# Attention scores from split q and k, with the transposes two steps behind, in a fused attention and feed-forward kernel

## The chip, the cores and the metric

The kernel runs on one core of a Trainium2 chip. The metric is device time in microseconds (us) of one execution. Three runs of the kernel before gave a median of 1192.46 us, between 1191.99 and 1193.89.

## What is computed

Attention over 4 batches and 8 heads of 576 positions and 64 dimensions with a learned bias of the relative position, and then two feed-forward parts over its 2304 x 512 result. All inputs are float32.

```python
def attn(q, k, v, w1, b1, w2):                  # (4, 8, 576, 64)
    scores = q @ k.T / 8
    x = log1p(abs(i - j)) / log1p(max(i, 1))
    bias = relu(x * w1 + b1) @ w2               # one 576 x 576 plane a head
    attn = softmax(scores + bias)
    return attn @ v
def moe1(x, w_in, w_out):                       # 512 -> 2048 -> 512
    h = x @ w_in
    return (h * cos(h)) @ w_out
def moe2(x, w_gate, w_val, w_out, rms_g):       # 512 -> 1536 -> 512
    xn = x / sqrt(mean(x * x) + 1e-6) * rms_g
    g = xn @ w_gate
    return (g * sigmoid(g) * (xn @ w_val)) @ w_out
```

## The kernel before

The program has three stages in one instruction order, which is written out by hand: each engine executes its instructions in the order in which the code issues them, and waits for the tiles of the others.

**Bias stage** (to about 72 us). In 36 steps T, VectorE (and ScalarE for one of some four) makes the hidden features `ft` of 16 positions (`features`, L413), TensorE multiplies them with w2, and the planes go to DRAM. Steps 0, 1 and 2 of the first attention unit lie at T = 28, 31 and 35 (`STEP_AT`).

**Attention** (to about 332 us). A unit u is a pair of heads and a batch, 16 in all, with five steps p (`step`, L328). Steps 0 to 3 treat 128 queries of both heads, step 4 the last 64 queries of both. `qk` multiplies q and k in float32 into one PSUM tile `psS` a head; there are two such tiles (L212). In steps 0 to 3 the two heads sit on different halves of TensorE's rows, so their instructions run in pairs; a float32 instruction shows as two in the trace. `softmax` adds the bias and takes the row minimum on VectorE (L231, here called a reduction), which frees the tile, and ScalarE takes the exponential (L235). `tr(u, p - 1)` then transposes the exponentials of the step before: four blocks that ScalarE copies out, four that VectorE copies out (L248) and a last one (L251, copied at L252), in PSUM tiles `pt` of three buffers. `av` multiplies five chunks of v with the transposed exponentials, for a half of the queries at a time (half 0: 256, half 1: 320), into the single PSUM tile `o`. `recip` makes the reciprocals of the sums (L287, L288), and GpSimd spreads them over `rw` (L290). `norm` transposes them on TensorE into a PSUM tile of the same three buffers (L298), and ScalarE copies them to `rbc` (L300). `norm_out` multiplies `o` with them on VectorE (L313), which frees `o`, and splits the result: ScalarE rounds it to `xh` (L315), GpSimd subtracts to get the rest, `xl` (L316).

**Feed-forward parts.** All products are of three rounded ones (`mm3`): the high part with the high, the high with the low, the low with the high part. The work is cut into items n: 80 of the first part (16 blocks of 128 features by 5 blocks of tokens) and 60 of the second (12 by 5). Item n makes its features, and item n - 2 (`LAG`) multiplies its own with the output weights.

**Weights.** They come as float64 in 68 pieces. A piece passes `w_dma`, `w_abs` (ScalarE, L105), `w_conv` (VectorE, in two halves of two instructions each: L116 and L117, L120 and L121) and `w_split` (ScalarE rounds at L137, GpSimd subtracts at L138) into a slot of a ring. Conversions are placed in steps 0 and 3 of the units from 4 on, and behind the items. `w_tick` decides what may be issued after a step or an item, from what was already done one call earlier:

```python
128         j = i % (WA + WB)
...
153         i = wstate["abs"]
154         if i < wstate["dmad"] and i < wstate["splitd"] + NW32:
155             w_abs()
```

The ring has WA + WB = 10 slots (`wA`, `wB`), and NW32 = 6 converted pieces may lie ahead of the splitting. `ready` issues all that is missing just ahead of the products that need it.

In a step the order of issue is: `norm_out` of the unit before (p 1 and 3), `qk`, `norm` (p 2 and 4), `softmax`, `tr`, `av`, loads of k and q for the next unit (p 1), and the conversion half (p 0 and 3).

Of the kernel before, what the change touches and what calls it, by code (L numbers as in the profile page):

```python
# [23 lines left out]
SPAN = 2 * S - 4  # L24
BLKS = [(0, 512), (512, 512), (2048, 256), (1024, 512), (1536, 512)]
# [5 lines left out]
WA = 1  # L31
WB = 9
NRAW = 2
NW32 = 6
# [17 lines left out]
def attn_moe(tc, qd, kd, vd, smallp, lrow, ident_d, wf1, wf2, rmsg, out):  # L52
# [117 lines left out]
    def load_k(u):  # L170
        if u < 16:
            hp, b = divmod(u, 4)
            kt = prep.tile([128, 640], F32, tag="k", name="kt", bufs=2)
            nc.sync.dma_start(kt, kd[b, hp])
            kq[u] = [kt, None]

    def load_q(u):
        if u < 16:
            hp, b = divmod(u, 4)
            qt_ = prep.tile([128, 640], F32, tag="q", name="qt", bufs=2)  # L180
            nc.sync.dma_start(qt_, qd[b, hp])
            kq[u][1] = qt_
# [24 lines left out]
    def qk(u, p):  # L207
# [15 lines left out]
        return [ps]
# [14 lines left out]
    def tr(u, p):  # L238
        s_ = st[u]
        e = s_["e"].pop(p)  # L240
        if p < 4:
            eT, q0 = (s_["eT0"], 128 * p) if p < 2 else (s_["eT1"], 128 * (p - 2))
            for c, ev in ((0, nc.scalar.copy), (2, nc.vector.tensor_copy)):
                pt = psA.tile([128, 512], F32, tag="tr", name="pt", bufs=3)
                for i in range(4):
                    k0 = 128 * (c + i // 2) + (S + 64) * (i % 2)
                    nc.tensor.transpose(pt[:, 128 * i:128 * i + 128], e[:, k0:k0 + 128], ident)  # L247
                ev(eT[:, 2 * c:2 * c + 4, q0:q0 + 128], pt.rearrange("p (c q) -> p c q", c=4))  # L248

            pt = psA.tile([128, 512], F32, tag="tr", name="pt", bufs=3)  # L250
            nc.tensor.transpose(pt[:, 0:128], e[:, 512:640], ident)  # L251
            nc.vector.tensor_copy(eT[:, 8, q0:q0 + 128], pt[:, 0:128])  # L252
        else:
            eT = s_["eT1"]
            pt = psA.tile([128, 512], F32, tag="tr", name="pt", bufs=3)
            for c in range(4):
                nc.tensor.transpose(pt[:, 128 * c:128 * c + 128], e[:, 128 * c:128 * c + 128], ident)  # L257
            nc.scalar.copy(eT[:, 0:8, 256:320], pt.rearrange("p (c q) -> p c q", c=8))
            pt = psA.tile([128, 512], F32, tag="tr", name="pt", bufs=3)
            nc.tensor.transpose(pt[:, 0:128], e[:, 512:640], ident)  # L260
# [545 lines left out]
```

## Time and profile before

| | |
|---|---|
| median of 3 runs | 1192.46 us |
| the profiled execution | 1192.12 us, span 1190.3 us |
| TensorE (PE) busy | 1173.7 us, 99% |
| VectorE (DVE) busy | 825.6 us, 69% |
| ScalarE (ACT) busy | 542.1 us, 46% |
| GpSimd (POOL) busy | 351.6 us, 30% |
| granted TensorE clock | full in all 40 slices |
| chain that ended last | PE 85%, DVE 8%, ACT 3%, issue 2%, DMA 1% |

The span is the time in which the profile saw the engines; the 1.8 us between it and the execution's own time lie around it. Busy shares are means over the three stages. The chain follows each piece of work back to what released it; its shares say which engine's work the end hung on. In the rows further below, an entry in square brackets is idle time just ahead of the instruction, and the instruction that ended it.

### The profile page before, as it was taken

Reading aid. Unit: us, or ns where it says so; the run is one execution under the profiler, and the core shown is the slowest. Engines: PE = TensorE matmul, PEld = TensorE weight load, DVE = VectorE, ACT = ScalarE, POOL = GpSimd, SP = SyncE. Lnnn points to the kernel's source line nnn. Section 1 sums busy time; section 2 is a strip of 40 time slices with the busy share of each in tenths; the row PEclk is TensorE's granted clock in tenths of the full one; section 3 lists DMA queues with packets and bytes.
Section 4 is the critical chain, followed back from the end, with each engine's and each line's share of the span. In section 5 each row is a group of like instructions: output and inputs, shape, how many; then the busy total and the mean of one; then the engine's idle time right before and its main releaser. Section 6 shows DMA issues by size and latency. Waiting matters only on the chain.

```text
span 1190.3 us, 17685 instructions
## 1 busy us (share of the span) xinstructions
PE 1173.7 (99%) x6628; PEld 907.4 (76%) x6628; DVE 825.6 (69%) x1588; ACT 542.1 (46%) x1060; POOL 351.6 (30%) x373
## 2 busy tenths in 40 slices
PE   7999999999999999999999999999999999999998
PEld 3466666666678888888888887888888888888887
DVE  8966677777778789879879987885565355533232
ACT  7966667767654444445435546332222222222111
POOL 0011112222232244234234445663331232123111
PEclk9999999999999999999999999999999999999999
DMA  6833425362212011201201110111112011200012
GB/s 194 267 120 108 135 66 160 103 191 65 69 37 70 19 36 36 71 19 37 70 18 43 46 36 18 50 58 36 36 36 74 16 46 43 71 1 1 36 46 78
DMA packets 30852, 79.23 MB, mean 67 GB/s; under 512 B 3888, under 2 KB 4144, under 8 KB 30768
## 3 DMA queue, kind: packets, MB, share of 16 engines
q1 hardware_dynamic: 30480, 77.52, 20.8%
q8 instruction: 52, 0.85, 0.3%
q10 hardware_dynamic: 288, 0.59, 0.1%
q14 instruction: 32, 0.26, 0.1%
HBM read 62.76 MB, written 15.34 MB: 66 GB/s over the span
## 4 chain that ended last, share of the span: by engine, by line
PE 85%; DVE 8%; ACT 3%; issue 2%; DMA 1%; POOL 0%; SPq 0%; DVEq 0%; ACTq 0%; POOLq 0%
PE y L508 25%; PE h L508 13%; PE hg L508 12%; PE hv L508 12%; PE o L278 7%; PE psS L217 6%; PE pt L247 5%; PE psS L222 1%; DVE ft L413 1%; PE psb L443 1%; ACT G L449 1%; DVE yacc L611 1%; PE pt L257 1%; PE rp L298 1%; PE pt L251 1%
## 5 line engine op out<-in xcount | busy, mean ns | idle before, releaser
L508 PE MATMUL y<-g,wB 128*128 128x512 f32 (+1 forms) x960 | 213.4, 370 | 1.7 <-DVE yacc L611 1.2
L508 PEld LDWEIGHTS y<-g,wB 128*128 128x128 f32 x960 | 167.6, 188 | 34.4 <-DVE yacc L611 2.8
L558 POOL TENSOR_TENSOR g<-t,g 128x512 fp32r<-128x512 f32 (+1 forms) x80 | 98.1, 1227 | 236.8 <-ACT g L557 236.8
L575 POOL TENSOR_TENSOR g<-t,g 128x512 fp32r<-128x512 f32 (+1 forms) x60 | 74.1, 1235 | 292.3 <-ACT g L574 292.3
L231 DVE CUSTOM_DVE_ANT_0 e<-psS,bias 128x576 f32<-128x576 f32 x144 | 103.8, 753 | 63.6 <-PE psS L217 47.7
L508 PE MATMUL h<-xh,wB 128*128 128x512 f32 (+1 forms) x480 | 145.4, 369 | 0.0
L508 PE MATMUL y<-wB,g 128*128 128x512 f32 x594 | 143.5, 390 | 0.0
L235 ACT ACTIVATE e<-e,sm 128x576 f32<-128x576 f32 x144 | 110.6, 769 | 53.1 <-DVE sm L231 53.1
L508 PE MATMUL hv<-xh,wB 128*128 128x512 f32 (+1 forms) x440 | 133.7, 369 | 0.0
L508 PE MATMUL hg<-xh,wB 128*128 128x512 f32 (+1 forms) x440 | 133.2, 368 | 0.4 <-DVE t L570 0.4
L570 DVE TENSOR_TENSOR t<-t,hg 128x512 f32<-128x512 f32 (+1 forms) x60 | 38.0, 633 | 137.4 <-ACT t L569 137.4
L508 PEld LDWEIGHTS y<-wB,g 128*128 128x128 f32 x594 | 110.8, 188 | 22.5
L569 ACT ACTIVATE t<-hg 128x512 f32<-128x512 f32 (+1 forms) x60 | 33.3, 554 | 168.0 <-PE hg L508 161.8
L574 ACT CAST g<-t 128x512 fp32r<-128x512 f32 (+1 forms) x60 | 34.7, 578 | 164.5 <-DVE t L573 164.5
L508 PEld LDWEIGHTS h<-xh,wB 128*128 128x128 f32 x480 | 87.8, 188 | 16.0 <-issue 0.5
L552 ACT ACTIVATE r<-r 128x512 f32<-128x512 f32 (+1 forms) x80 | 47.2, 590 | 108.0 <-DVE r L549 107.7
L278 PE MATMUL o<-eT,v 128*64 128x256 f32 (+1 forms) x640 | 94.3, 416 | 0.0
L508 PEld LDWEIGHTS hg<-xh,wB 128*128 128x128 f32 x440 | 80.5, 188 | 15.0 <-DVE t L570 0.9
L138 POOL TENSOR_TENSOR wB<-w,wB 128x512 fp32r<-128x512 f32 x61 | 85.2, 1403 | 21.4 <-ACT wB L137 21.4
L508 PEld LDWEIGHTS hv<-xh,wB 128*128 128x128 f32 x440 | 80.6, 188 | 13.7
L557 ACT CAST g<-t 128x512 fp32r<-128x512 f32 (+1 forms) x80 | 46.2, 578 | 96.3 <-DVE t L556 87.9
L508 PE MATMUL h<-xl,wB 128*128 128x512 f32 (+1 forms) x240 | 88.4, 368 | 0.0
(116 smaller groups left out, 2130.8 us busy)
## 6 DMA issues: line engine op xcount, KB each, us to landing
raw<-in_wf_dram SPq DMA_DIRECT2D x68, 512.0 KB, 3.5
bdram<-G SPq DMA_DIRECT2D x36, 288.0 KB, 3.6
bias<-bdram SPq DMA_DIRECT2D x32, 288.0 KB, 3.3
kt<-in_kd_dram SPq DMA_DIRECT2D x16, 320.0 KB, 4.5
qt<-in_qd_dram SPq DMA_DIRECT2D x16, 320.0 KB, 5.1
v<-in_vd_dram SPq DMA_DIRECT2D x16, 320.0 KB, 3.9
out_dram<-yacc SPq DMA_DIRECT2D x16, 256.0 KB, 2.1
bias<-bdram SPq DMA_DIRECT2D x4, 144.0 KB, 3.3
```

What stands on the lines that cost most here:

```text
L138: eng.tensor_tensor(t[:, 1, :], r, t[:, 0, :].bitcast(F32), op=ALU.subtract)
L217: nc.tensor.matmul(pss[hh][:, x, 0:288], qt_[r, 128 * p:128 * p + 128], kt[r, k0:k0 + 288], start=True, stop=True, tile_position=(64 * hh, 0))
L231: nc.vector.tensor_tensor_reduce(out=e.rearrange("p (a b) -> p a b", a=2), in0=ps[:, :, 0:288], in1=bias_t[j].rearrange("p (a b) -> p a b" ...
L235: nc.scalar.activation(e, e, AF.Exp, bias=s_["m"][:, j:j + 1], scale=-1.0, accum_out=s_["sum"][:, j:j + 1])
L247: nc.tensor.transpose(pt[:, 128 * i:128 * i + 128], e[:, k0:k0 + 128], ident)
L278: nc.tensor.matmul(o[64 * hh:64 * hh + 64, 0:n], vt[:, c, 64 * hh:64 * hh + 64], eT[:, 2 * c + (hh if c < 4 else 0), :], start=(c == 0), s ...
L508: nc.tensor.matmul(ps, a, b_, start=(first and k == 0), stop=(last and k == tot - 1))
L552: nc.scalar.activation(r, r, AF.Abs)
L557: nc.scalar.copy(g[:, 0, :tn], t)
L558: nc.gpsimd.tensor_tensor(g[:, 1, :tn], t, g[:, 0, :tn].bitcast(F32), op=ALU.subtract)
L570: nc.vector.tensor_tensor(t, t, pg, op=ALU.mult)
L575: nc.gpsimd.tensor_tensor(g[:, 1, :tn], t, g[:, 0, :tn].bitcast(F32), op=ALU.subtract)
```

## The change

- *Scores.* GpSimd splits k and q of the next unit into a rounded and a rest part (`split`: a cast and a subtraction over 128 x 640 each), k in step 2, q in step 3. `qk` then sums three rounded products. Unit 0 keeps its float32 products, and unit 1 is loaded and split at T = 2 of the bias stage.
- *Transposes.* `tr` is two steps behind the scores and cut in two: its first four transposes and ScalarE's copy ahead of the softmax, the rest behind it.
- *Reciprocals.* They are transposed into the free columns of the tile of the last transpose (steps 2 and 4), and VectorE copies them out instead of ScalarE. `norm_out` moves to steps 2 and 4, and `xt` has one buffer instead of two.
- *Products with v.* They follow in steps 4 (chunks 0 and 1), 0 (2 and 3) and 1 (4) for half 0, and in 2 (0 to 2) and 3 (3 and 4) for half 1.
- *Loads.* k and q of the next unit are issued in step 0.
- *Weights.* The ring keeps ten slots, of which three (`wC`) exist only from item 2 on; until then seven pieces may be split. NW32 is 5.

```diff
+TERMS = ((0, 0), (0, 1), (1, 0))
...
-WB = 9
+WB = 6
+WC = 3
+RING = WA + WB + WC
-NW32 = 6
+NW32 = 5
...
-        j = i % (WA + WB)
+        j = i % (WA + WB + WC)
...
+        elif j >= WA + WB:
+            t = wstate["wc"].tile([128, 2, 512], F32R, tag="w", name="wC", bufs=WC)
...
+    def load(u):
+        for k, src in enumerate((kd, qd)):
+            if u == 0:
+                t = rawp.tile([128, 512, 2], I32, tag="raw", name="first", bufs=NRAW)
+                t = t.rearrange("p a b -> p (a b)")[:, 0:640].bitcast(F32)
+                kq[0] = kq.get(0, []) + [t]
+            else:
+                t = prep.tile([128, 640], F32, tag="raw", name="raw" + "kq"[k], bufs=2)
+            nc.sync.dma_start(t, src[u % 4, u // 4])
+            raw_kq[u, k] = t
+
+    def split(u, k):
+        raw = raw_kq.pop((u, k))
+        t = prep.tile([128, 2, 640], F32R, tag="kq"[k], name="kq"[k] + "t", bufs=2)
+        nc.gpsimd.tensor_copy(t[:, 0, :], raw)
+        nc.gpsimd.tensor_tensor(t[:, 1, :], raw, t[:, 0, :].bitcast(F32), op=ALU.subtract)
+        kq[u] = kq.get(u, []) + [t]
...
         kt, qt_ = kq[u]
-        if p < 4:
...
+        terms = TERMS
+        if u == 0:
+            terms, kt, qt_ = ((0, 0),), kt.unsqueeze(1), qt_.unsqueeze(1)
+        pss = [psB.tile([128, 2, 512], F32, tag="S", name="psS", bufs=2) for _ in range(2 if p < 4 else 1)]
+        for x in range(2):
+            for n, (a, b_) in enumerate(terms):
+                for hh, ps in enumerate(pss):
+                    r = slice(64 * hh, 64 * hh + 64) if p < 4 else slice(0, 128)
...
+                    nc.tensor.matmul(ps[:, x, 0:288], qt_[r, a, 128 * p:128 * p + 128], kt[r, b_, k0:k0 + 288],
+                                     start=(n == 0), stop=(n == len(terms) - 1), tile_position=(64 * hh, 0))
+        return pss
...
-    def tr(u, p):
+    def tr(u, p, first, spread=None):
         s_ = st[u]
-        e = s_["e"].pop(p)
+        if first and p in (0, 2):
...
+        pt = psA.tile([128, 512], F32, tag="tr", name="pt", bufs=3)
+        if first:
+            for i in range(4):
+                k0 = 128 * (i // 2) + (S + 64) * (i % 2) if p < 4 else 128 * i
+                nc.tensor.transpose(pt[:, 128 * i:128 * i + 128], e[:, k0:k0 + 128], ident)
+            nc.scalar.copy(eT[:, 0:512 // n, q0:q0 + n], pt.rearrange("p (c q) -> p c q", q=n))
+            return
...
+            for i in range(4):
+                k0 = 128 * (2 + i // 2) + (S + 64) * (i % 2)
+                nc.tensor.transpose(pt[:, 128 * i:128 * i + 128], e[:, k0:k0 + 128], ident)
+            nc.vector.tensor_copy(eT[:, 4:8, q0:q0 + n], pt.rearrange("p (c q) -> p c q", q=n))
+        nc.tensor.transpose(pt[:, 0:128], e[:, 512:640], ident)
+        if spread is not None:
+            norm(*spread, pt[:, 128:384])
...
-    def norm(u, half):
+    def norm(u, half, rp):
         s_ = st[u]
-        rp = psA.tile([128, 512], F32, tag="tr", name="rp", bufs=3)
...
-        nc.scalar.copy(rbc[:, 0:256], rp[:, 0:256])
+        nc.vector.tensor_copy(rbc[:, 0:256], rp)
         s_["rbc", half] = rbc
...
-        xt = ap.tile([128, 320], F32, tag="xt", name="xt", bufs=2)
+        xt = ap.tile([128, 320], F32, tag="xt", name="xt", bufs=1)
...
-        if u > 0 and p in (1, 3):
-            norm_out(u - 1, p // 2)
+        if u > 0 and p in (2, 4):
+            norm_out(u - 1, p // 4)
-        if p == 2 and u > 0:
-            norm(u - 1, 1)
+        if p == 3 and u > 0:
             norm_tail(u - 1)
-        if p == 4:
-            norm(u, 0)
+        back = (u, p - 2) if p > 1 else (u - 1, p + 3)
+        if back[0] >= 0:
+            tr(*back, True)
...
-        if p > 0:
-            tr(u, p - 1)
+        if back[0] >= 0:
+            tr(*back, False, (u, 0) if p == 4 else (u - 1, 1) if p == 2 and u > 0 else None)
+        if p == 2:
+            recip(u, 0)
+        if p == 0 and u > 0:
+            recip(u - 1, 1)
+        if p == 4:
+            av(u, 0, [0, 1])
         elif u > 0:
-            tr(u - 1, 4)
-            av(u - 1, 0, [3, 4])
-        if p == 1 and u > 0:
-            av(u - 1, 1, [0, 1, 2])
-        if p == 2:
-        if p == 4:
-            av(u, 0, [2])
-        if p == 3:
-            av(u, 0, [0, 1])
+            av(u - 1, p // 2, ([2, 3], [4], [0, 1, 2], [3, 4])[p])
+        if p in (2, 3) and 0 < u < 15:
+            split(u + 1, p - 2)
+        if p == 0 and 0 < u < 15:
+            load(u + 1)
...
-        if T == 20:
-            load_k(1)
-        if T == 22:
-            load_q(1)
+        if T == 2:
+            load(1)
+            split(1, 0)
+            split(1, 1)
...
-        w_tick(lambda i: i < WA + WB or lastuse[pieces[i - WA - WB]] <= n - SPL,
+        w_tick(lambda i: i < WA + WB or n > 1 and (i < RING or lastuse[pieces[i - RING]] <= n - SPL),
                nsplit=2 if n < 6 or m == 2 else 1)
...
-    tr(15, 4)
+    tr(15, 3, True)
+    tr(15, 3, False)
     recip(15, 1)
-    av(15, 0, [3, 4])
+    av(15, 0, [2, 3, 4])
+    tr(15, 4, True)
+    tr(15, 4, False, (15, 1))
...
+    wstate["wc"], st_wc = pool("wc")
```

How this stands on TensorE, from step 4 of a unit through steps 0 and 1 of the next to the scores of step 2 (`psS` scores, `pt` transposes, `rp` reciprocals, `o` products with v). Before:

```order
L298 MATMUL rp<-ident,rw 128x128 x2
L247 MATMUL pt<-ident,e 128x128 x8
L251 MATMUL pt<-ident,e 128x128
L278 MATMUL o<-eT_1806,v 64x256 x2
L217 MATMUL psS<-kt,qt 128x288 x4
L257 MATMUL pt<-ident,e 128x128 x4
L260 MATMUL pt<-ident,e 128x128
L278 MATMUL o<-eT_1806,v 64x256 x4
L217 MATMUL psS<-kt,qt 128x288 x4
```

Now:

```order
L311 MATMUL pt<-ident,rw 128x128 x2
L292 MATMUL o<-eT_2005,v 64x256 x4
L231 MATMUL psS<-kt,qt 128x288 x12
L259 MATMUL pt<-ident,e 128x128 x4
L265 MATMUL pt<-ident,e 128x128 x4
L268 MATMUL pt<-ident,e 128x128
L292 MATMUL o<-eT_2005,v 64x256 x4
L231 MATMUL psS<-kt,qt 128x288 x12
L259 MATMUL pt<-ident,e 128x128 x4
L268 MATMUL pt<-ident,e 128x128
L292 MATMUL o<-eT_2005,v 64x256 x2
L231 MATMUL psS<-kt,qt 128x288 x12
```

Between the scores of step 1 (the second row with `psS` x12) and those of step 2 stand now five transposes and two products with v (a pair); before, four products stood there behind the five transposes, in step 0. The separate tile of the reciprocals is gone.

On VectorE, from the normalization of one half to the scores of step 4 (`ISA` is the reduction, `xt` the normalization, `w_…` the conversion of a weight piece). Before:

```order
L313 TENSOR_TENSOR xt<-o,rbc 128x320
L231 ISA e,sm<-psS,bias_2274 128x576
L231 ISA sm 128x1
L231 ISA e,sm<-psS,bias_2278 128x576
L231 ISA sm 128x1
L248 COPY eT_2861<-pt 128x4x128
L252 COPY eT_2861<-pt 128x128
L120 SCALAR_TENSOR_TENSOR w_2695<-raw,w_2695 128x512
L121 SCALAR_TENSOR_TENSOR w_2695<-raw,w_2695 128x512
L231 ISA e,sm<-psS,bias_2322 128x576
L231 ISA sm 128x1
```

Now:

```order
L241 ISA e,sm<-psS,bias_2536 128x576
L241 ISA sm 128x1
L241 ISA e,sm<-psS,bias_2540 128x576
L241 ISA sm 128x1
L266 COPY eT_3176<-pt 128x4x128
L272 COPY eT_3176<-pt 128x128
L123 SCALAR_TENSOR_TENSOR w_3032<-raw,w_3032 128x512
L124 SCALAR_TENSOR_TENSOR w_3032<-raw,w_3032 128x512
L326 TENSOR_TENSOR xt<-o,rbc 128x320
L241 ISA e,sm<-psS,bias_2589 128x576
```

The normalization stood ahead of step 3's reductions and stands now behind the conversion, ahead of step 4's reduction.

On ScalarE, at items 83 and 84 (`t` and `g` the item's own work, `wA` and `wB` the rounding of a piece, L668 and L670 the output of the normalization between the two parts). Before:

```order
L569 ACTIVATE t<-hg 128x256
L574 CAST g<-t 128x256
L137 CAST wA<-w_7319 128x512
L105 ACTIVATE w_7705<-raw 128x512
L670 CAST xh<-yacc 128x512 x2
L660 COPY rb<-rbp 128x512
L569 ACTIVATE t<-hg 128x256
L574 CAST g<-t 128x256
L137 CAST wB<-w_7503 128x512
L105 ACTIVATE w_7779<-raw 128x512
L569 ACTIVATE t<-hg 128x256
L574 CAST g<-t 128x256
```

Now:

```order
L567 ACTIVATE t<-hg 128x256
L572 CAST g<-t 128x256
L108 ACTIVATE w_8295<-raw 128x512
L668 CAST xh<-yacc 128x512 x2
L658 COPY rb<-rbp 128x512
L567 ACTIVATE t<-hg 128x256
L572 CAST g<-t 128x256
L142 CAST wA<-w_8096 128x512
L108 ACTIVATE w_8369<-raw 128x512
L567 ACTIVATE t<-hg 128x256
L572 CAST g<-t 128x256
L142 CAST wB<-w_8295 128x512
```

The rounding of the piece that goes into `wA` stood behind item 83's `g` and stands now behind item 84's.

## Rows read from the trace of the kernel before

**Rows 1.** Chain of waits, 75 to 320 us, its sum by engine, tile and line.

```profile
by line: PE o L278 31.6%; PE psS L217 27.5%; PE pt L247 22.1%; PE psS L222 6.7%; PE rp L298 3.4%; PE pt L257 3.4%; PE pt L251 3.2%; PE o L273 1.6%; PE pt L260 0.6%; issue 0.0%
```

**Rows 2.** Timeline of TensorE, units 7 to 8: start us, us, engine, line, operation, count.

```profile
203.17 1.24 PE L217 MATMUL psS<-kt,qt 64*128 64x288 f32 x8
204.34 1.09 PE L247 MATMUL pt<-ident,e 128*128 128x128 f32 x8
...
206.49 1.24 PE L222 MATMUL psS<-kt,qt 128*128 128x288 f32 x4
...
203.52 0.41 PE L217 MATMUL psS<-kt,qt 64*128 64x288 f32 x2
...
204.00 0.41 PE L217 MATMUL psS<-kt,qt 64*128 64x288 f32 x2
```

**Rows 3.** Chain of waits, 315 to 400 us: start us, us, engine, tile, line, count.

```profile
330.52 0.58 PE o L278 x4
...
331.80 1.01 PE o L278 x8
...
375.25 1.43 PE h L508 x12
```

**Rows 4.** TensorE's weight loads by line and shape: busy us, mean ns | idle before, releaser.

```profile
L251 PEld LDWEIGHTS pt<-ident,e 128*128 128x128 f32 x64 | 9.0, 141 | 2.1 <-ACT rbc L300 2.1
```

**Rows 5.** Timeline of all engines, 200 to 218 us, [idle before <- releaser].

```profile
201.47 0.75 DVE L231 CUSTOM_DVE_ANT_0 e<-psS,bias 128x576 f32<-128x576 f32 x1
...
201.94 1.30 PE L278 MATMUL o<-eT,v 128*64 128x320 f32 x8
...
202.15 0.69 DVE L248 COPY eT<-pt 128x512 f32<-128x512 f32 x1
...
202.75 0.28 DVE L252 COPY eT<-pt 128x128 f32<-128x128 f32 x1
...
203.48 0.40 POOL L290 COPY rw<-sm 128x256 f32<-128x256 f32 x1 [5.03 <-DVE sm L288]
...
206.60 0.68 DVE L120 SCALAR_TENSOR_TENSOR w<-raw,w 128x512 int32<-128x512 int32 x1
...
212.54 0.81 PEld L217 LDWEIGHTS psS<-kt,qt 64*128 64x128 f32 x8 [0.39 <-DVE sm L231]
...
213.22 0.39 DVE L116 TENSOR_SCALAR w<-w 128x512 f32<-128x512 f32 x1
...
213.73 1.09 PE L247 MATMUL pt<-ident,e 128*128 128x128 f32 x8
...
216.75 1.24 PE L217 MATMUL psS<-kt,qt 64*128 64x288 f32 x8
```

**Rows 6.** Timeline of VectorE, then of GpSimd, 428.5 to 433 us.

```profile
430.81 1.66 DVE L121 SCALAR_TENSOR_TENSOR w<-raw,w 128x512 int32<-128x512 int32 x1
...
430.19 1.74 POOL L138 TENSOR_TENSOR wB<-w,wB 128x512 fp32r<-128x512 f32 x1
```

**Rows 7.** Timeline of VectorE in the bias stage, 38 to 80 us.

```profile
37.75 11.67 DVE L413 TENSOR_SCALAR ft<-L,nbp 128x576 f32<-128x576 f32 x27
```

**Rows 8.** Timeline around items 82 to 84 and item 112.

```profile
752.01 1.52 DVE L120 SCALAR_TENSOR_TENSOR w<-raw,w 128x512 int32<-128x512 int32 x1
...
753.03 0.48 PE L508 MATMUL hv<-xh,wB 128*128 128x512 f32 x1
...
768.87 2.81 PE L508 MATMUL y<-wA,g 128*128 128x512 f32 x11 [0.96 <-POOL wA L138]
...
773.56 0.66 PE L633 MATMUL ssp<-ident,sq 128*128 128x128 f32 x4 [0.45 <-DVE sq L627]
...
774.18 0.62 ACT L137 CAST wB<-w 128x512 fp32r<-128x512 f32 x1
...
992.15 0.39 PE L508 MATMUL hg<-xh,wB 128*128 128x512 f32 x1
...
992.77 1.47 POOL L138 TENSOR_TENSOR wB<-w,wB 128x512 fp32r<-128x512 f32 x1
```

More of the change, by code (lines that the diff above doesn't have):

```diff
@@ L168, in attn_moe @@
     vts = {}
[L170 to L182, printed above, removed]
+    raw_kq = {}
+    def load(u):
[14 more added lines that the diff above has]
+        kq[u] = kq.get(u, []) + [t]
     bias_t = {}
@@ L237, in softmax @@
             nc.gpsimd.tensor_copy(e2[:, S:S + 64], e2[:, S - 64:S])
-    def tr(u, p):
+    def tr(u, p, first, spread=None):
         s_ = st[u]
-        e = s_["e"].pop(p)
-        if p < 4:
[L242 to L248, printed above, removed]
-            pt = psA.tile([128, 512], F32, tag="tr", name="pt", bufs=3)
-            nc.tensor.transpose(pt[:, 0:128], e[:, 512:640], ident)
-            nc.vector.tensor_copy(eT[:, 8, q0:q0 + 128], pt[:, 0:128])
-        else:
[L254 to L260, printed above, removed]
-            nc.vector.tensor_copy(eT[0:64, 8, 256:320], pt[0:64, 0:64])
-            nc.vector.tensor_copy(eT[64:128, 8, 256:320], pt[64:128, 64:128])
@@ new lines, in tr @@
+        if first and p in (0, 2):
+            s_["eT", p // 2] = ap.tile([128, 9, 256 + 32 * p], F32, tag=f"eT{p}", name=f"eT{p}", bufs=1)
+        e = s_["e"][p]
+        eT, q0 = s_["eT", min(p // 2, 1)], 128 * (p % 2 if p < 4 else 2)
+        n = 128 if p < 4 else 64
+        pt = psA.tile([128, 512], F32, tag="tr", name="pt", bufs=3)
[5 more added lines that the diff above has]
+            return
@@ L264, in av @@
+        if p < 4:
+            nc.vector.tensor_copy(eT[:, 8, q0:q0 + n], pt[:, 0:128])
+        else:
+            for r in (slice(0, 64), slice(64, 128)):
+                nc.vector.tensor_copy(eT[r, 8, q0:q0 + n], pt[r, r])
+        del s_["e"][p]
     def av(u, half, cs):
@@ L266, in av @@
         n = 256 if half == 0 else 320
-        eT = s_["eT0"] if half == 0 else s_["eT1"]
+        eT = s_["eT", half]
         if cs[0] == 0:
@@ L425, in attn_moe @@
     nc.vector.tensor_copy(cv[:, 1:2], pc[:, 0:1])
-    load_k(0)
-    load_q(0)
+    load(0)
     nc.sync.dma_start(ident, ident_d)
@@ L715, in rest @@
     def rest():
-        norm(15, 1)
         norm_out(15, 0)
@@ L731, in attn_moe @@
     env["mp2"], st_mp2 = pool("mp2")
+    wstate["wc"], st_wc = pool("wc")
     for n in range(2, NI + LAG):
         run_item(n)
-    for s in (st_mp2, st_yp, st_psY, st_mp, st_x, st_wb, st_psH, st_raw, st_wa, st_const):
+    for s in (st_wc, st_mp2, st_yp, st_psY, st_mp, st_x, st_wb, st_psH, st_raw, st_wa, st_const):
         s.close()
```

22 lines of the change are left out of this document (removed).

## The prediction

> **What bounds the kernel now.** I read the page for the order of the stages, then the chain of waits over the attention, then TensorE alone in time, then VectorE and GpSimd in the same steps, then the few places of the feed-forward part where TensorE stops. The chain from 75 to 320 us is TensorE from end to end, "issue" 0.0% [rows 1]: nothing but its own instruction stream sets the pace there. One step's scores are eight instructions, side by side in pairs. The second pair starts at 203.52 and the fourth at 204.00, so a pair takes 0.24 us; from the first score to the first transpose it is 1.17 us [rows 2], which is 4 x 0.242 and 0.20 for filling the array and changing its layout. VectorE's reductions follow each other at 0.68 us (201.47, 202.15) and the big copy of transposes takes 0.60 (to 202.75) [rows 5]. VectorE has slack everywhere except where step 0 goes over into step 1: there the next scores were held until VectorE had released their PSUM tile (212.54, 0.39 <- DVE) [rows 5]. The feed-forward part is TensorE too, with few stops.
>
> **The change part by part.** The sum is made against the profiled execution, 1192.12 us, which is 0.34 below the median of 1192.46.
>
> *Scores.* Two-part full-precision instructions become three rounded products. Twelve rounded products of 256 columns take 1.43 us [rows 3], 0.119 each with their loads, so 288 columns cost about 0.133. The trace shows no rounded product on half the array. Bounds: 0.119, as if 256 wide, and 0.242, the pair it replaces. I take 0.133, because the present half-array pairs already run together. Then 6 x 0.133 + 0.20 = 1.00 against 1.17: 0.17 less in each of 5 steps of 15 units (unit 0 keeps its form), **-12.7**.
>
> *Reciprocals.* The fifth-chunk transposes waited 2.1 us in all for ScalarE's copy of the reciprocals [rows 4]. That copy now shares their tile: **-2.0**. It moves to VectorE; between a 128-wide and a 512-wide copy I price it 0.35, once in step 2 and once in step 4, counted below.
>
> *Step 1 becomes short.* After step 1's scores TensorE now has only five transposes and two pairs with v. The row before 331.80 shows 0.70 for the former (from 330.52 + 0.58) and 0.58 for the latter [rows 3]: 1.28 us. VectorE's two reductions start 0.10 after the transposes, at 0.68 intervals, and the second frees its tile about 0.81 after its start: 1.59. So step 2's scores wait 0.32. From unit 6 a conversion half (L116, 0.39 at 213.22 [rows 5], and L117, of the same kind: 0.9 with the gaps) stands in VectorE's step 0. There VectorE needs 0.10 + 1.36 + 0.60 + 0.6 (small copy, reciprocals) + 0.9 = 3.56 us. TensorE's step 0 was 3.32 (203.17 to 206.49 [rows 2] has the same work) and becomes 3.15. VectorE is about 0.3 late and the wait 0.6. 5 x 0.32 + 10 x 0.6: **+7.6**. Bounds 0 (an earlier release) and 12.
>
> *Step 4 waits for the o tile.* The normalization of the second half moves from the head of step 3 to the head of step 4, behind step 3's conversion half on VectorE, and the first product with v of step 4 can't start before it, since o has one buffer. From the first transpose of step 2 as zero: VectorE does two reductions, big copy, the new 0.35 copy; 0.73 after the small copy begins GpSimd copies the reciprocals (202.75 to 203.48, then 0.40) [rows 5]: to 3.54. Behind that copy stand four GpSimd instructions, casting and subtracting k and q, 128x640 each. A subtraction of 512 columns takes 1.47 at 992.77 [rows 8]; I take 1.6 for 640, with 1.84, its rate, as the upper bound. A cast isn't shown; the plain copy of 256 columns is 0.40, so between 0.4 and 1.0: I take 0.75, as part of a copy is fixed. They end at 8.25. TensorE: 3.02 from transposes to scores with this much work on v (213.73 to 216.75) + 0.22 for two more transposes + 1.00 of scores, so step 3's transposes begin at 4.24, and VectorE reaches the conversion (0.68 an instruction, 206.60) 2.25 later, at 6.49, in the midst of the four. TensorE wants the o tile at 4.24 + 1.13 + 1.23 (201.94 to 203.17 [rows 2, 5]) + 0.90 + 1.29 = 8.79. Undisturbed, VectorE has released it at 6.49 + 1.4 + 0.5 = 8.4: 0.4 of slack.
>
> It is not undisturbed. L121 is of the same kind and size as L120, which takes 0.68 at 206.60 [rows 5]; at 430.81 it took 1.66, ending 0.54 after GpSimd's instruction that had begun at 430.19 [rows 6]; L120 itself took 1.52 at 752.01 [rows 8]. The Trainium skill, SBUF — State Buffer, section "SBUF: two separate sides", gives the rule: VectorE with two SBUF inputs or in a two-port mode and GpSimd take a shared port pair for a whole instruction, and the loser fully blocks. The trace agrees: 1.66 for 0.68. By that rule the term below stands; without it the term is nothing.
>
> So the first conversion instruction waits out the cast (to 6.65, then 0.54), the second a whole subtraction (to about 8.65, then 0.54), and o is free at 9.7: 0.9 late. If the first meets a subtraction instead, it is 2.1 late. I take 1.0 for units 6 to 14: **+9.0**, bounds 0 and 19.
>
> *Unit 1's split in the bias stage.* VectorE's features run without a gap, 27 in 11.67 us, 0.43 each [rows 7], an instruction on SBUF alone. Four GpSimd instructions of 4.7 us fall among them. At most VectorE loses all 4.7; at least nothing, if GpSimd gives way or ScalarE hides it. Step 1's transposes and their copies leave this stage, 0.9 us of VectorE. I take **+2.5**.
>
> *Two steps behind.* Those transposes (1.13) and a pair of chunks with v (0.58) now fall after the bias stage, where TensorE has no idle time: **+1.7**.
>
> *Fewer converted weights.* The table of weight pieces keeps ten slots but only five converted pieces ahead. In the order of the instructions three pieces now come late. Piece 39 (item 82): its conversion is now the one that VectorE begins at 752.01. L120 took 1.52 there, so with L121 behind it (0.68) it would end at 754.2; with ScalarE's cast (0.62 at 774.18) and GpSimd's 1.47 behind, the products start at 756.3, not 753.03: 3.3 late. Piece 40 (item 84) is now cast where the cast at 774.18 stands, behind that item's g; with 0.62 and 1.47 it is ready at 776.3, and the products that ran from 768.87 are 7.4 late in all, less the 0.45 that TensorE waited at 773.56: +7.0, in which the 3.3 are contained, since that g came late through VectorE. Piece 56 (item 112) takes the place that piece 57 had on GpSimd, 992.77 + 1.47 = 994.24, and its products began at 992.15: +2.1 [rows 8]. **+9.1**, bounds 4 and 11. The 7 instead of 9 pieces ready at the end of the attention cost nothing: the eighth is wanted four items later.
>
> Extra loads cost nothing: they are the same bytes, issued up to a step earlier. Sum: -12.7 - 2.0 + 7.6 + 9.0 + 2.5 + 1.7 + 9.1 = +15.2, **1207.3 us**.
>
> **The rivals.** *(A) TensorE's stream stays the only limit of the attention.* This one ends faster. Its one point is VectorE's place in time: if VectorE is never behind by more than its slack (0.4 us before the o tile, none before the short step), the waits of 7.6, 9.0 and 2.5 are zero and -12.7 - 2.0 + 1.7 + 9.1 = -3.9: 1188.2. For it speaks that TensorE hardly ever waits for VectorE now [rows 1]; against it the 0.39 at 212.54, with 0.43 us more work on TensorE before it than there will be.
>
> *(B) GpSimd gives way.* VectorE's back-to-back instructions keep the port and GpSimd waits. Then 9.0 and 2.5 go and +3.7 is left: 1195.8. Against it is 430.81.
>
> *(C) Half-array rounded products don't hide their weight loads.* A pair then costs at worst the 0.242 of today: 6 x 0.242 + 0.20 = 1.65, 0.48 more over 75 steps, +36; the waits for VectorE vanish: +36 - 2.0 + 2.5 + 1.7 + 9.1 gives 1239.4. Against it: 1.43 us for twelve, each with a new load into the same rows [rows 3]. The Trainium skill, TensorE: Matmul & The Clock Gate, section "The mechanism", says that a load overlaps running products only where its row group differs, which speaks for this rival. By that rule the time is 1239.4; the trace doesn't agree, with 0.119 us a product.
>
> **How the numbers follow.** Forecast 0.66, A 0.15, B 0.15, C 0.04. The forecast's own bounds: low, with 4 for the o tile, 0 for the bias stage and 5 for the weights, +3.6 (1195.7); high, with 19, 4 and 11, +28.6 (1220.7). The range 1187 to 1218 reaches down to A and leaves out C, the edge below A and the top of the forecast, under 2 in 10. 0.2% is 2.4 us, about what a measurement of this kernel can tell from no change. Faster: A and a little of the forecast's low edge, 0.16. Same: half of B, 0.08. Slower: the rest, 0.76.
>
> **What would show it.** Right: step scores of about 1.0 us; in units 6 to 14, 18 us from one step-4 score to the next where it was 17.3, and in units 1 to 5 16.6 where it was 17.1; waits of TensorE for the normalization in step 4 and for VectorE's reductions in step 2; conversion instructions of 1.2 us and more in the attention; stops of 3 us or more at items 82 and 84 and 2 at item 112. Wrong: scores of 1.4 us or more (C), conversions of 0.7 in the attention (B), no TensorE wait for VectorE there (A), or no longer stop at the change to the second feed-forward part.

## The result, and the profile after

The changed kernel takes 1203.40 us, the median of four runs (1202.79 to 1206.87), against 1192.22 (1191.80 to 1193.89) for the kernel before: a ratio of 1.0097, 95% interval 1.0075 to 1.0119. The forecast was 1207.3, with a range of 1187 to 1218 and slower as the likeliest side. The profiled execution took 1202.98 us; its span is 1201.2, 10.9 more than before, and TensorE lost two points of its busy share although it executes fewer busy microseconds. The page, first part:

```profile
span 1201.2 us, 18222 instructions
...
PE 1168.1 (97%) x6898; PEld 919.9 (77%) x6898; DVE 851.2 (71%) x1620; ACT 533.1 (44%) x1028; POOL 455.6 (38%) x433
```

The two traces can be laid over each other at the scores and at the items, which gives the difference by stage:

| place | before | after | difference |
|---|---|---|---|
| unit 1, step 0: first score | 70.84 | 72.59 | +1.75 |
| unit 15, step 4: last score | 328.69 | 328.48 | -0.21 |
| item 0: first product | 332.75 | 334.24 | +1.49 |
| item 80: its first step on ScalarE | 740.18 | 741.14 | +0.96 |
| item 100 | 892.59 | 901.94 | +9.35 |
| item 139 | 1181.06 | 1191.66 | +10.59 |

The first row in the two traces, before and then now (TensorE's timeline: start us, us, engine, line):

```profile
70.84 0.75 PE L217 MATMUL psS<-kt,qt 64*128 64x288 f32 x2
```

```profile
72.59 0.40 PE L231 MATMUL psS<-kt,qt 64*128 64x288 f32 x1
```

It is where unit 0's step 4 ends; the expectations further below call this point "unit 0's step 4". That step's own first score comes at 67.89 before and at 68.76 now, so that half of the 1.75 arises in the bias stage and half in the step, which has two more products with v (0.43 us) and a wait of 0.33 for one of VectorE's copies.

Between items 87 and 111 the difference is 9.35 throughout, and from 112 on 10.59. So the attention gained 2.0 us only, its two ends cost 1.75 and 1.70, of which 0.5 came back, and the second feed-forward part lost 9.6 at two places. TensorE's waits after, all engines that it waited for (total us, times, longest):

```profile
PE o L292 <- DVE xt L326: 6.9, 9, 1.0
...
PE y L506 <- ACT wA L142: 3.5, 1, 3.5
...
PE hv L506 <- ACT wC L142: 1.7, 1, 1.7
...
PE y L506 <- POOL wA L143: 1.0, 1, 1.0
PE hg L506 <- POOL wB L143: 0.9, 1, 0.9
...
PE hv L506 <- POOL wC L143: 0.6, 1, 0.6
```

The first row is the wait for the normalization, nine times, in units 6 to 14: before, no row names `xt`. The other five are weights that come late; before, only the fourth was there, at item 84 [rows 8]. From step 3 of unit 8 to step 2 of unit 9 (timeline: start us, us, engine, line):

```profile
204.40 0.72 POOL L191 CAST qt<-rawq 128x640 fp32r<-128x640 f32 x1
...
205.14 0.68 DVE L123 SCALAR_TENSOR_TENSOR w<-raw,w 128x512 int32<-128x512 int32 x1
205.19 2.04 POOL L192 TENSOR_TENSOR qt<-rawq,qt 128x640 fp32r<-128x640 f32 x1
...
205.85 1.93 DVE L124 SCALAR_TENSOR_TENSOR w<-raw,w 128x512 int32<-128x512 int32 x1
...
207.71 0.48 DVE L326 TENSOR_TENSOR xt<-o,rbc 128x320 f32<-128x320 f32 x1
...
208.25 1.08 PE L292 MATMUL o<-eT,v 128*64 128x256 f32 x8 [0.74 <-DVE xt L326]
...
209.26 1.06 PE L231 MATMUL psS<-kt,qt 64*128 64x288 f32 x12
...
210.25 0.65 PE L259 MATMUL pt<-ident,e 128*128 128x128 f32 x4
...
212.40 1.07 PE L231 MATMUL psS<-kt,qt 64*128 64x288 f32 x12
...
214.68 1.52 PE L231 MATMUL psS<-kt,qt 64*128 64x288 f32 x12
```

VectorE's second conversion instruction (L124) takes 1.93 us, where the same instruction took 0.69 before (VectorE's timeline of the kernel before, at the same place):

```profile
207.32 0.69 DVE L121 SCALAR_TENSOR_TENSOR w<-raw,w 128x512 int32<-128x512 int32 x1
```

It ends 0.55 after GpSimd's subtraction of q (205.19 + 2.04 = 207.23), `xt` follows it, and TensorE waits 0.74 for `xt`. Step 0's scores take 0.99 from the first of them to the first transpose (209.26 to 210.25), for 1.17 before [rows 2]. The last two rows are the scores of steps 1 and 2: the same twelve products take 1.07 and 1.52. The second is the wait for the reductions, and it hides inside the scores: only one head's tile is free, so that the first product starts at 214.68 by itself and the other eleven follow from 215.15 on, and for most of that time TensorE counts as busy.

In the second feed-forward part, TensorE's timeline at items 82 and 84, and then the same trace by stretches (stretch, its length, busy us and count of PE, PEld, DVE, ACT and POOL, then the granted clock, the DMA share and GB/s):

```profile
755.93 0.50 PE L506 MATMUL hv<-xh,wC 128*128 128x512 f32 x1 [1.73 <-ACT wC L142]
...
757.29 0.94 PE L506 MATMUL hv<-xh,wC 128*128 128x512 f32 x2 [0.62 <-POOL wC L143]
...
776.54 0.49 PE L506 MATMUL y<-wA,g 128*128 128x512 f32 x1 [3.45 <-ACT wA L142]
778.05 4.38 PE L506 MATMUL y<-wA,g 128*128 128x512 f32 x11 [1.02 <-POOL wA L143]
```

```profile
753.00:755.00 2.00, 1.20 (x8) 0.80 (x6) 1.97 (x3) 0.00 (x0) 0.96 (x1) 1.00 0.00 0
758.00:760.00 2.00, 2.00 (x6) 1.59 (x5) 1.56 (x5) 0.00 (x0) 0.20 (x1) 0.50 0.04 16
778.00:780.00 2.00, 1.95 (x5) 1.56 (x6) 0.69 (x1) 0.00 (x0) 0.00 (x0) 0.53 0.00 0
```

TensorE stops for 1.73 and 0.62 us, then for 3.45 and 1.02, and after each of the two stops it runs at the lower of its two levels (1.2 of 2.4 GHz) for a while: 0.50 of the clock from 758 to 760, 0.53 from 778 to 780. The eleven products at 778.05 take 4.38 us where 2.81 stood [rows 8].

### The profile page after: what moved, and what is told of

The parts are those of the page before. It is cut to its first block, busy times and chain, and to the rows that moved or that the text cites. A ratio compares the mean times of both kernels' runs of the same rounds, so it can differ in the third digit from the quotient of the medians.

```text
span 1201.2 us, 18222 instructions
## 1 busy us (share of the span) xinstructions
PE 1168.1 (97%) x6898; PEld 919.9 (77%) x6898; DVE 851.2 (71%) x1620; ACT 533.1 (44%) x1028; POOL 455.6 (38%) x433
## 4 chain that ended last, share of the span: by engine, by line
PE 65%; DVE 9%; ACT 2%; issue 1%; POOL 1%; DVEq 0%; ACTq 0%; POOLq 0%
PE y L506 25%; PE h L506 13%; PE hv L506 12%; PE hg L506 11%; PE o L292 1%; PE psS L231 1%; DVE yacc L609 1%; DVE e L241 1%; DVE t L546 1%; DVE w L123 1%; DVE r L547 1%; DVE t L545 1%; DVE t L554 1%; DVE w L124 1%; DVE sq L625 1%
## 5 line engine op out<-in xcount | busy, mean ns | idle before, releaser
L506 PE MATMUL y<-g,wB 128*128 128x512 f32 (+1 forms) x600 | 133.4, 370 | 1.3 <-DVE yacc L609 1.2
L506 PEld LDWEIGHTS y<-g,wB 128*128 128x128 f32 x600 | 105.0, 188 | 21.6 <-DVE yacc L609 2.5
L506 PE MATMUL hv<-xh,wB 128*128 128x512 f32 (+1 forms) x320 | 97.1, 369 | 0.0
L231 PEld LDWEIGHTS psS<-kt,qt 64*128 64x128 f32 (+1 forms) x810 | 64.8, 185 | 37.2 <-DVE sm L241 10.2
L506 PE MATMUL y<-wB,g 128*128 128x512 f32 x378 | 91.4, 390 | 0.0
L231 PE MATMUL psS<-kt,qt 64*128 64x288 f32 (+1 forms) x810 | 85.4, 311 | 2.1 <-DVE sm L241 1.3
L506 PEld LDWEIGHTS y<-wB,g 128*128 128x128 f32 x378 | 70.5, 188 | 14.4
L571 DVE TENSOR_TENSOR t<-t,hv 128x512 f32<-128x512 f32 (+1 forms) x60 | 38.0, 633 | 60.7 <-PE hv L506 60.4
L506 PE MATMUL y<-g,wC 128*128 128x512 f32 (+1 forms) x360 | 79.9, 370 | 0.1
L260 ACT COPY eT<-pt 128x512 f32<-128x512 f32 x80 | 46.8, 585 | 65.3 <-PE pt L259 65.3
```

The source lines that it names most:

```text
L231: nc.tensor.matmul(ps[:, x, 0:288], qt_[r, a, 128 * p:128 * p + 128], kt[r, b_, k0:k0 + 288], start=(n == 0), stop=(n == len(terms) - 1), ...
L260: nc.scalar.copy(eT[:, 0:512 // n, q0:q0 + n], pt.rearrange("p (c q) -> p c q", q=n))
L506: nc.tensor.matmul(ps, a, b_, start=(first and k == 0), stop=(last and k == tot - 1))
L571: nc.vector.tensor_tensor(t, t, pv, op=ALU.mult)
```

## The experiments

The theory after the result: three things make up the loss, and each has its own cause. The five converted pieces make the weights late; GpSimd's splitting holds VectorE's conversion and through it the normalization; step 1 is too short for two reductions. The rivals are named with the runs.

### Six converted pieces, in a smaller ring

```diff
-WB = 6
-WC = 3
+WB = 5
+WC = 4
...
-NW32 = 5
+NW32 = 6
```

> The changed kernel with six converted pieces ahead instead of five (WB 5, WC 4: still ten slots, six of them before item 2). Theory (the fifth-instead-of-sixth converted piece makes pieces 39, 40 and 56 late): the stops of TensorE at items 82, 84 and 112 go, about 9.6 us less, 1193.8 us. Rival (the ring, with three slots that come only at item 2, makes them late): the stops stay, about 1203 us.

1202.65 us, ratio 1.0080 (1.0063 to 1.0097). The time says rival, the trace says otherwise. No stop is left at items 82, 84 and 112: from item 80 on the difference to the kernel before stays between 9.55 and 9.60. But there is a new one, at item 3 (TensorE's timeline, and the granted clock behind it):

```profile
353.73 0.79 PE L506 MATMUL h<-xh,wC 128*128 128x512 f32 x1 [5.46 <-ACT wC L142]
...
355.79 1.22 PE L506 MATMUL h<-xh,wC 128*128 128x512 f32 x2 [0.83 <-POOL wC L143]
```

```profile
355.00:360.00 5.00, 4.21 (x10) 3.35 (x11) 0.00 (x0) 0.00 (x0) 1.96 (x2) 0.50 0.00 0
```

With six pieces ready instead of seven, item 3's first weights are split only at item 2. On ScalarE the difference to the kernel before is 0.15 us at item 2, ahead of the stop, and 9.7 from item 20 on, of which 6.3 are the stop and most of the rest products at the lower clock level (0.50 from 355 to 360 us). So the stops of item 82 and later are made by NW32, and seven pieces, of which the prediction said that they cost nothing, are just enough.

### Five converted pieces in the kernel before

```diff
-NW32 = 6
+NW32 = 5
```

> The kernel before with NW32 5 instead of 6 and nothing else. Theory: the same stops appear at items 82, 84 and 112 and nothing changes ahead of item 82: about 9.6 us more than before, 1201.8 us. Rival (ring): no stops, 1192 us.

1202.04 us, ratio 1.0073 (1.0056 to 1.0090): this one line costs nearly as much as the whole change. Up to item 80 TensorE's trace is that of before (within 0.2 us); behind item 112 it is 10.2 late. TensorE's waits:

```profile
PE y L508 <- ACT wA L137: 4.6, 1, 4.6
...
PE hv L508 <- ACT wB L137: 1.7, 1, 1.7
...
PE hg L508 <- POOL wB L138: 0.9, 1, 0.9
```

They are the rows of the changed kernel with another ring. The rival falls.

### No splits

```diff
-        if p in (2, 3) and 0 < u < 15:
-            split(u + 1, p - 2)
-        if p == 0 and 0 < u < 15:
-            load(u + 1)
+        if p == 3 and 0 < u < 15:
+            kq[u + 1] = kq[u]
```

> The changed kernel without the splits and loads of k and q of units 2 to 15, which all use unit 1's (so the scores of those units are left out). Theory (GpSimd's casts and subtractions hold VectorE's conversion up, and that the normalization): the second conversion instruction of step 3 takes 0.7 us instead of 1.8, TensorE's waits for the normalization in step 4 (6.9 us in all) go, step 4 takes 3.21 us in all units, about 1196 us. Rival (VectorE is late by the conversion alone): the waits stay within 1 us of 6.9 in all, about 1203 us. In both the waits inside step 2's scores stay, 0.33 and 0.47 us a unit.

1195.99 us, ratio 1.0026 (1.0017 to 1.0035). The wait for `xt` is gone, step 4 is 3.21 us in all units, and the conversion has its old length (VectorE by line and shape, 160 to 325 us, first without the splits, then in the changed kernel):

```profile
L124 DVE SCALAR_TENSOR_TENSOR w<-raw,w 128x512 int32<-128x512 int32 x10 | 6.9, 693 | 0.3
```

```profile
L124 DVE SCALAR_TENSOR_TENSOR w<-raw,w 128x512 int32<-128x512 int32 x9 | 17.4, 1932 | 0.3
```

0.693 against 1.932: it is GpSimd, not the conversion's place. The loads of k and q, which this run leaves out too, aren't it either: the run with float32 scores below has the loads and no splits, and there the instruction takes 0.69. The wait in step 2 stays, with 0.33 and 0.47, as expected of both. The time agrees within 0.1 us with what the theory gave.

### Float32 scores in the new order

```diff
-        terms = TERMS
-        if u == 0:
-            terms, kt, qt_ = ((0, 0),), kt.unsqueeze(1), qt_.unsqueeze(1)
+        terms, kt, qt_ = ((0, 0),), kt.unsqueeze(1), qt_.unsqueeze(1)
...
-        if p in (2, 3) and 0 < u < 15:
-            split(u + 1, p - 2)
```

(`load` writes into the tiles of k and q.)

> The changed kernel with float32 scores in all units and no split: the new order of transposes and products alone. Theory (three rounded products save 0.17 to 0.19 us in each of 75 steps): 13 to 14 us more than the run without splits, less the 1.7 us that unit 1's split cost in the bias stage, about 1208 us. Rival (the scores' saving is lost to VectorE, which paces the steps): within 5 us of the run without splits, about 1197 us.

1203.97 us, ratio 1.0087 (1.0068 to 1.0107). Against the run without splits that is 8.0 us more, not 12: between the theory's number and the rival's. What is clean is the step: from the scores of step 4 to those of step 0 and on to step 1, first with float32, then with rounded products.

```profile
207.82 1.24 PE L230 MATMUL psS<-rawk,rawq 128*128 128x288 f32 x4
...
211.21 1.24 PE L230 MATMUL psS<-rawk,rawq 64*128 64x288 f32 x8
...
214.52 1.24 PE L230 MATMUL psS<-rawk,rawq 64*128 64x288 f32 x8
```

```profile
204.54 1.06 PE L231 MATMUL psS<-kt,qt 128*128 128x288 f32 x6
...
207.75 1.06 PE L231 MATMUL psS<-kt,qt 64*128 64x288 f32 x12
...
210.89 1.06 PE L231 MATMUL psS<-kt,qt 64*128 64x288 f32 x12
```

3.39 and 3.31 against 3.21 and 3.14. Steps 1 and 3 give 0.18 and 0.19, and step 2, where VectorE paces it, 0.17 in units 1 to 5 and 0.03 after. So three rounded products save 0.18 a step, with half the array too, and 0.14 of it is lost again in step 2 of ten units. The rest of the miss lies at the start. With nothing split, the first score of unit 1 comes at 69.73, against 72.00 in the run without the later splits and 72.59 in the changed kernel: unit 1's split alone costs the bias stage 2.3 to 2.9. And in the run without splits, step 0 of unit 1 took 4.42 us from the end of the wait inside its scores, and step 1 took 2.53, where the later units have 3.14 and 2.27. The granted clock stood at its lower level there (0.50, the last number but two):

```profile
76.00:78.00 2.00, 2.00 (x10) 0.76 (x8) 1.33 (x6) 1.52 (x4) 0.40 (x1) 0.50 0.00 0
```

The five steps' savings are 0.89 a unit: 15 x 0.89, less 1.4 of step 2, 2.3 of the bias stage and 1.5 of unit 1, is 8.1, against the 8.0 measured. That is closer than the sum deserves: float32 had the longer wait inside unit 1's first scores, and counted with it unit 1 lost 1.0 and the sum is about 8.6, where the two traces are 8.5 apart at the first score of unit 15's step 4.

### A chunk more in step 1

```diff
-            av(u - 1, p // 2, ([2, 3], [4], [0, 1, 2], [3, 4])[p])
+            av(u - 1, p // 2, ([2], [3, 4], [0, 1, 2], [3, 4])[p])
```

> The changed kernel with chunk 3 of the first half's products with v in step 1 instead of step 0. Theory (step 1 is too short for VectorE's two reductions): step 1 becomes 0.58 us longer, step 0 as much shorter, and the wait inside step 2's scores (0.33 us) goes in units 2 to 6; in the later ones, where VectorE comes late out of step 0 already, 0.47 us stay. About 1.6 us less, 1201.8 us. Rival (the wait is made in step 2 itself): no change, 1203.4 us; second rival (all of the wait is step 1's length): it goes in all units, 1197 us.

1202.19 us, ratio 1.0086 (1.0071 to 1.0101), 1.2 less; the times alone would not tell that from nothing, the steps do. (The profiled execution, at 1202.71, hardly shows it in sum: steps 0 and 1 of unit 1 took 9.04 us in it, 1.9 more than in the changed kernel, with the granted clock at 0.50 from 76 to 78 us.) Step 2 was 4.55 us in units 1 to 5 and is 4.23; from unit 6 on it was 4.69 and is 4.70. The scores of step 2 in unit 11:

```profile
246.70 1.05 PE L231 MATMUL psS<-kt,qt 64*128 64x288 f32 x12
...
249.39 1.54 PE L231 MATMUL psS<-kt,qt 64*128 64x288 f32 x12
```

1.54 us still, against 1.05 in step 1. The theory holds for the early units: step 1's length was the cause. That VectorE carries its lateness over from step 0 in the later ones, where the conversion half stands, is not shown by this run; the run with all of it, which moves that half, shows it.

### Unit 1's split later in the program

```diff
         if T == 2:
             load(1)
-            split(1, 0)
-            split(1, 1)
+        if T == NTT - 2:
+            split(1, 0)
+            split(1, 1)
```

> The changed kernel with the split of unit 1's k and q behind the last features, at T = 34 instead of 2. Theory (GpSimd's cast, which the trace shows for 32.3 us from 17.68 on, waits while VectorE's features follow each other without a gap, and once it is in, three features take 0.97 to 1.79 us instead of 0.51): the cast takes 0.7 to 1.0 us, no feature is longer than 0.6 us, unit 0's step 4 begins 1.7 us earlier, 1201.7 us. Rival (what the stage lost is the order of the transposes): same time, 1203.4 us; or unit 1 waits for its k and q and the time is 1 to 3 us longer.

1203.77 us, ratio 1.0101 (1.0084 to 1.0117): nothing. The edit did not do what it said. GpSimd has no other work in the stage, so the cast is the next instruction in its queue wherever the program issues it, and it starts with the data at 17 us as before. It says nothing of the cause; what the cast does there is under the last heading.

### Early splits and six converted pieces

```diff
-NW32 = 5
+NW32 = 6
...
+                t = prep.tile([128, 640], F32, tag="raw", name="raw" + "kq"[k], bufs=1)
...
         if p == 2:
+            if 0 < u < 15:
+                split(u + 1, 1)
+            if u < 14:
+                load(u + 2, (0,))
             recip(u, 0)
         if p == 0 and u > 0:
             recip(u - 1, 1)
+            if u < 15:
+                split(u + 1, 0)
+                load(u + 1, (1,))
...
-        if p in (2, 3) and 0 < u < 15:
-            split(u + 1, p - 2)
-        if p == 0 and 0 < u < 15:
-            load(u + 1)
...
         if T == 2:
-            load(1)
+            load(1, (0,))
             split(1, 0)
+            load(1, (1,))
             split(1, 1)
```

> The changed kernel with six converted pieces ahead, paid with one raw tile for k and q instead of two (7 pieces still ready before item 2), and the splits at steps 0 (k) and 2 (q, ahead of the reciprocals) instead of 2 and 3. Theory: no stop at items 3, 82, 84 or 112 (9.6 us less) and no wait for the normalization in step 4, as GpSimd is idle when step 3's conversion runs (7.4 less): 1186.4 us. Rival (the port is only wanted elsewhere now: k's split meets the conversion half of step 0): L119 and L120 take over 1 us, the wait inside step 2's scores grows, 1190 to 1199 us.

1192.42 us, ratio 1.0005 (0.9996 to 1.0014): 6 us over the theory. In the attention and behind it everything is as the theory had it: step 4 is 3.21 us again (one of 3.55 apart), step 2 is 4.69 as it was, L124 takes 0.69, and the difference to the kernel before does not change by more than 0.1 from item 40 to the end. The 6 us are one stop in the bias stage (timeline of GpSimd, SyncE and TensorE):

```profile
18.54 9.93 POOL L192 CAST kt<-rawk 128x640 fp32r<-128x640 f32 x1 [14.20 <-DMA rawk<-in_kd_dram]
...
30.11 0.33 SPq L186 DMA_DIRECT2D rawq<-in_qd_dram  x1
30.53 6.77 SPq L452 DMA_DIRECT2D bdram<-G  x8
...
34.93 5.68 PE L445 MATMUL psb<-ft,small 128*32 128x512 f32 x52 [9.70 <-ACT G L451]
```

With one raw tile the load of q waits on SP's queue for GpSimd to have split k, and behind it on that queue stand eight transfers of bias planes. GpSimd's cast takes 9.93 us, because VectorE's features leave it no gap; the planes' tiles run out, and TensorE waits 9.70 for ScalarE's next one. The first score of unit 1 comes at 79.14 instead of 72.59: 6.55 late, and 1192.4 - 6.5 is the 1186 of the theory. The rival falls: nothing moved to step 0.

### All of it

```diff
-            av(u - 1, p // 2, ([2, 3], [4], [0, 1, 2], [3, 4])[p])
+            av(u - 1, p // 2, ([2], [3, 4], [0, 1, 2], [3, 4])[p])
...
-        if u >= 4 and p in (0, 3):
+        if u >= 4 and p in (3, 4):
...
         if T == 2:
             load(1, (0,))
+        if T == NTT - 2:
             split(1, 0)
             load(1, (1,))
             split(1, 1)
```

> The run with the early splits, and in it chunk 3 in step 1, unit 1's split at T = 34, and the conversion halves in steps 4 and 3 instead of 0 and 3. Theory (the terms add: 1.7 for the bias stage, 0.33 a unit for step 1, 0.14 a unit for the half of step 0): no wait inside step 2's scores, a unit of 16.2 us, about 1179 us. Rival (VectorE is late elsewhere: in step 4, which now has a conversion half): a wait of 0.3 us or more a unit in step 0 or 1, 1184 us or more.

1179.35 us, ratio 0.9898 (0.9883 to 0.9912), within 0.4 of the theory's 1179, but not by all of its terms. A unit is 16.18 us (two of them 16.4), step 2 4.23 in all units: with the conversion half in step 4, VectorE no longer comes late. The load of q now stands late enough on SP's queue to stop nothing, but the first score of unit 1 comes at 73.78, 1.2 later than in the changed kernel and not 1.7 earlier, since the split of q ends at 71.3 only and the reciprocals are copied behind it. So the agreement is in part luck; the four times lie between 1178.38 and 1181.98.

### Nothing split in the bias stage

```diff
-            if u == 0:
-                t = rawp.tile([128, 512, 2], I32, tag="raw", name="first", bufs=NRAW)
...
+            if u < 2:
+                t = prep.tile([128, 2, 640], F32R, tag="kq"[k], name="kq"[k] + "t", bufs=2)[:, 0, :].bitcast(F32)
...
-        if u == 0:
+        if u < 2:
...
-            if u < 15:
+            if 0 < u < 15:
                 split(u + 1, 0)
...
         if T == 2:
-            load(1, (0,))
-        if T == NTT - 2:
-            split(1, 0)
-            load(1, (1,))
-            split(1, 1)
+            load(1)
```

> The last run with float32 scores in unit 1 as in unit 0, so that nothing is split in the bias stage. Theory (GpSimd's split costs VectorE's features 2.5 us and unit 1 a late start, which moving it in the program could not cure): unit 0's step 4 begins near 70 us instead of 73.8, unit 1's steps are 0.17 us longer each, in all some 2.5 to 3 us less, about 1176.5 us. Rival (the late start is hidden by the transposes behind it): the same 1179 us within 1 us.

1177.47 us (1177.39 to 1177.74), ratio 0.9879 (0.9862 to 0.9895), 14.4 us under the kernel before: the best of the runs. The first score of unit 1 comes at 69.54, 1.3 earlier than before the change. The end comes 2.7 us earlier than in the run above, and 1.9 by the times. Its page, first part:

```profile
span 1175.3 us, 18179 instructions
...
PE 1158.6 (99%) x6880; PEld 915.6 (78%) x6880; DVE 834.2 (71%) x1620; ACT 532.8 (45%) x1028; POOL 417.2 (36%) x429
```

TensorE is back at 99% with 15 us less of span.

## Why the prediction was right, point by point

The direction, the three places and their causes were right, and the measured +10.9 of the span stands against +15.2. Most losses came out smaller than forecast. Term by term:

| term | forecast | measured | from |
|---|---|---|---|
| scores | -12.7 | -13.4 | 0.17 to 0.19 a step, float32 against rounded in one order, 75 steps |
| reciprocals | -2.0 | -2.0 | no wait at the last transposes is left [rows 4] |
| step 1 short | +7.6 | +6.4 | 0.33 in 5 units, 0.47 in 10 |
| o tile | +9.0 | +7.5 | 0.8 in 8 units, 1.0 in one |
| unit 1's split in the bias stage | +2.5 | +1.75 | first score of unit 1 |
| two steps behind | +1.7 | +1.2 | +1.7 from the last score to item 0, 0.5 of it given back |
| weights | +9.1 | +9.6 | 8.4 at items 82 to 84, 1.2 at item 112 |
| sum | +15.2 | +11.1 | |

*Scores.* 0.133 a pair for products on half the array was taken from full-array products, and it holds: 0.18 a step against the forecast 0.17. A step's scores take 0.99 us to the first transpose, where the prediction had 1.00 and rival C, loads that aren't hidden, 1.65. The rule of the Trainium skill, TensorE: Matmul & The Clock Gate, section "The mechanism", that a load overlaps only where row groups differ, isn't what these rows show: six products of the same row group, each with its own load, fit into that 0.99.

*Step 1 becomes short.* The mechanism was right and its size a little high in the later units: 0.47 for 0.6. That the wait shows inside the scores and not ahead of them was not forecast; whoever looks for idle TensorE finds only part of it.

*The o tile.* The case that the prediction worked out, 0.9 a unit, is the one that the trace shows: the first conversion instruction starts where the cast has just ended and takes 0.68, and only the second waits, for the whole subtraction. The 1.0 that was taken made room for the other case, in which the first one meets a subtraction; no unit shows it, and a step 4 became 0.8 longer (1.0 in unit 13, where the first instruction took 0.89). Rival B, GpSimd gives way, is out in the attention and, unexpectedly, half true in the bias stage (below). Rival A is out by nine waits for `xt`.

*Weights.* The sum is right for a reason that is half wrong. Waits grew by 5.0 us at items 82 and 84 (6.8 after, 1.9 before), not 7.0. The other 3.4 are the clock: products behind each stop at the lower level, such as item 84's eleven in 4.38 for 2.81, a term that the prediction didn't have. Item 112 cost 1.2 and not 2.1, and the two errors nearly offset each other, which is luck. Piece 39 was ready in full at 757.29, which without the 0.96 that the kernel already lagged is the forecast 756.3; piece 40, at 778.05, was 0.8 later than forecast.

*Seven ready pieces cost nothing*: right, but with no room, as the run with six shows.

*The bias stage.* The +1.75 is the difference of two numbers: the split cost 2.3 to 2.9, and the stage's lost transposes gave 1.1 back (69.73 without the split, 70.84 before). Counted from unit 0's first score, which lies between 47.46 and 47.99 in these runs, the split cost 2.6 to 2.7 and 0.9 came back; 0.9 is what the prediction had for the second.

*What would show it.* Three of the signs that were named came out smaller. From one step 4 to the next, units 6 to 14 took 17.5 us and not 18 (units 1 to 5 took 16.5 for 16.6); only the second of the two conversion instructions passed 1.2; and the stops at items 82 and 112 were 2.4 and 0.9, not 3 and 2.

## What to carry to other kernels

When memory is taken from a staging buffer, count what stands ahead of the far end of the program: one converted piece fewer cost 10 us in the last third of the program, two thirds of what the change saved elsewhere. Work that is put on an idle engine is not free if it holds up an instruction of the engine whose lateness matters, as GpSimd's subtraction did here with VectorE's conversion (1.93 us for 0.69); put it where the other has no such instruction in hand. And a forecast by terms lets each be tested by itself: here the losing terms could be undone one by one, and what was left of the change gained 14 us.

## What the runs showed that was not expected

GpSimd can be kept out for as long as VectorE leaves no gap. In the bias stage of the changed kernel (GpSimd's timeline):

```profile
17.68 32.27 POOL L191 CAST kt<-rawk 128x640 fp32r<-128x640 f32 x1 [12.90 <-DMA rawk<-in_kd_dram]
50.04 1.57 POOL L192 TENSOR_TENSOR kt<-rawk,kt 128x640 fp32r<-128x640 f32 x1
51.55 0.95 POOL L191 CAST qt<-rawq 128x640 fp32r<-128x640 f32 x1
```

A cast that takes 0.72 in the attention took 32.27 us here, from 17.68 to 49.95. VectorE's features follow each other at 0.43 us with 0.51 each, one overlapping the next, as before [rows 7]; the first other work of VectorE, a reduction at 49.29, let the cast in. In the five other runs that have this split and whose features were not stopped the same cast took 30.4 to 32.5 us, and 9.93 in the one where they were. Behind the reductions GpSimd's other three instructions fell among the features, and three of these took 1.28, 0.97 and 1.79 us, together 2.5 more than three of 0.51, nearly all of what the split cost (VectorE's timeline, now and then before):

```profile
49.29 0.75 DVE L241 CUSTOM_DVE_ANT_0 e<-psS,bias 128x576 f32<-128x576 f32 x1
...
50.64 4.73 DVE L412 TENSOR_SCALAR ft<-L,nbp 128x576 f32<-128x576 f32 x5
```

```profile
50.70 1.80 DVE L413 TENSOR_SCALAR ft<-L,nbp 128x576 f32<-128x576 f32 x4
```

The Trainium skill, SBUF — State Buffer, section "SBUF: two separate sides", has the lock go to whichever starts first, for a whole instruction; that agrees with the conversions in the attention (0.68 and 1.93), while a chain of overlapping instructions kept the port as a whole.

A stop of TensorE can cost more than its length: behind the stops at items 82 and 84, and behind the one at item 3 in the run with six pieces, the granted clock stood at its lower level, 1.2 GHz, for some microseconds, and that cost about half of the stops again (3.4 us for 6.8, some 3 for 6.3). It need not: behind the 0.94 at item 112 and the nine waits for `xt` the clock stayed full. The wait inside unit 1's first scores went either way: after 1.32 us of it in the changed kernel the clock stayed full, after 1.34 in the run without splits it fell.
